# A transformer block on one core: second norm modulated on its turned rows, and the work behind the last block in another order

## The chip, the cores and the metric

The kernel runs on one core of a Trainium2 chip. The metric is device time in microseconds (us) of one execution. Where one execution is profiled, its span (first to last instruction) is a little shorter than its time.

The engines: PE (TensorE, matmuls and turns, that is transposes), DVE (VectorE), ACT (ScalarE), POOL (GpSimd) and SP (SyncE, which here only issues DMAs). Each works through its own instructions in the order of the program; they wait for each other by semaphores. An engine's DMA issues stand in that same order.

## The reference, cut to what matters

2048 tokens of width 512, 32 query heads of 16 that share one key and one value head, and a hidden layer of 1792:

```python
mod = (_silu(c) @ w_mod).reshape(c.shape[0], 6, 1, -1)
sa, ca, ga, sb, cb, gb = (mod[:, 0], mod[:, 1], mod[:, 2], mod[:, 3], mod[:, 4], mod[:, 5])
h = _layernorm(x, axis=-1) * (1 + ca) + sa
x = x + ga * _A_ref(h, A_wq, A_wk, A_wv, A_wo)     # attention, softmax over all keys
h = _layernorm(x, axis=-1) * (1 + cb) + sb
x = x + gb * _B_ref(h, B_w1, B_w2)                 # relu(h @ w1) @ w2
return x
```

The change is about the second norm's `(1 + cb)` and `sb`, one number of each per column of the 512, and about what follows it for the last tokens.

## The kernel before

All arithmetic is float32. Where two operands are multiplied in the faster format (`float32r`), each is split into a high and a low part, and three products are added (`thrice`, line 536: high by high, high by low, low by high). `split` (line 272) makes the parts of a staged value: ACT copies the high part, POOL subtracts it to leave the low one.

**The head** (up to about 130 us) loads x and the weights, makes the six rows of the modulation, the first norm, the keys and values, and the first maxima. `mod_all` (line 218) makes one row of the modulation: PE multiplies silu(c) by a sixth of w_mod into a bank, ACT copies it to `mrow`, PE multiplies by a matrix of constants that adds the parts up and spreads the sum over all partitions, and ACT copies it out (line 225). For sb and cb this gives `sbr` and `cbr`, 128 x 512 each. For the first norm there is another way, `mod_col` (line 228): PE turns `mrow`, and a DVE reduction leaves in `cols` one number per partition and group of 128 columns. `tr1` uses those as scale and shift as turned rows leave their bank.

**The loop** goes over 8 blocks of 256 tokens by 4 groups of 8 heads, so 32 units, each of 16 tiles of keys. For each tile PE makes scores (`scores`, line 773), ACT takes exp, and PE multiplies by the values into the bank `ps_pv`. Maxima of a later unit (`max_of`, line 481) run beside them on PE and DVE. A hand-written row of letters (`PARTS`) says in what order PE gets these pieces; the letters `l` and `u` are portions of other work, which `behind(b)` (line 575) gives out: while block b + 1 is in the loop, the output projection, second norm and hidden layer of block b go in small portions into the bank `ps_fill`. In `behind`, POOL normalises two tiles of 128 tokens and multiplies and adds `cbr` and `sbr` (`normed`, lines 544 to 549); PE turns them; `turned_too` (line 580) copies the turned rows out by ACT and puts off `split` to a later place (`put_off`). Pieces of w1 (`w1s`, 512 KB each with both parts, 14 of them, three buffers) come from DRAM, where the head has left them split.

When a unit's values are done, `normalise` (line 782) makes the quotient: ACT copies the bank to `pvs`; numerators and sums are brought to matching partitions by DMA (`num`, `den`), DVE takes the reciprocal and POOL multiplies into `on` (in the profile under line 1005, where it is called, the last unit's under 1016, DVE's reciprocal too). In the last unit POOL copies both, and SP issues four DMAs for `num` and then four for `den` (lines 793 to 800).

**Behind the loop** first come 24 matmuls that are left of block 6's second layer (first tile of 128 tokens). Then `behind_last(7)` (line 651) does block 7, in the order in which it is written:

- it asks for x and three pieces of w1 (`open_block`, `load_w1`); each further piece is asked for when a chunk of the first layer has been given out (line 704) and waits for one of the three buffers
- it splits the heads' output in two halves of two groups each (`parts`, line 674: ACT high, DVE low), and gives PE 12 matmuls of block 6's second tile (`more(12)`)
- per tile of 128 tokens: 12 matmuls of the projection over the four groups, DVE adds x, takes the statistics (`ln_sums`), makes the reciprocal root in small operations on one column per partition (`ln_stats`, lines 253 to 261), and `normed` follows, the first tile on DVE, the second on POOL
- `more(99)` gives PE the other 30 matmuls of block 6, and DVE closes that tile (`close_block`)
- PE turns the normed rows (8 turns), `parts` splits them into `hh` and `hl`, and the first layer follows: 14 chunks of 12 matmuls (`dense1`), and `parts` with relu
- the second layer takes 84 matmuls, both tiles by turns, and DVE closes both tiles at the end.

Of the kernel before, what the change touches and what calls it, by code (L numbers as in the profile page):

```python
# [13 lines left out]
OP = mybir.AluOpType  # L14
# [29 lines left out]
PARTS = "cbcuaucuautcuau", "tbldldladbllbld"  # L44
SYNC = mybir.DependencyInfo(mybir.DependencyClass.Sync, mybir.DependencyReason.DATA)
# [15 lines left out]
def build(tc, nc, cst, sb, ps, dr, x, wq, wk, wv, wo, w1, w2, c, w_mod, out):  # L61
# [64 lines left out]
    cols = cst.tile([P, 2, DC], F32, name="cols")  # L126
    sbr = cst.tile([P, D], F32, name="sbr")
    cbr = cst.tile([P, D], F32, name="cbr")
# [89 lines left out]
    def mod_all(i, dst):  # L218

        pt = ps_fill()  # L220
        row = mod_row(i, pt)
        yield
        pt = ps_fill()
        nc.tensor.matmul(pt, mean, row, start=True, stop=True)
        nc.scalar.activation(dst, pt, AF.Copy, bias=1.0 if i == 4 else 0.0)
        yield
# [317 lines left out]
    def normed(x1, xn, ts, nm, y, eng):  # L544
        for n, t in enumerate(ts):
            eng.tensor_scalar(xn[:, t], x1[:, t], nm[:, n:n + 1], y[:, n:n + 1],
                              op0=OP.add, op1=OP.mult)
            eng.tensor_tensor(xn[:, t], xn[:, t], cbr, op=OP.mult)
            eng.tensor_tensor(xn[:, t], xn[:, t], sbr, op=OP.add)
# [25 lines left out]
    def behind(b):  # L575
# [74 lines left out]

    def behind_last(b):
# [5 lines left out]
        def second(t):  # L657
            pt = ps_fill()
            for d in dense2(b - 1, t, pt):
                on_all(d)  # L660
                yield
            close_block(b - 1, t, pt)

        before = second(1)
# [20 lines left out]
        for t in range(TT):  # L685
            pt = ps_exp()
            run_all(out_proj(pt, oo, t))
            V.tensor_tensor(x1[:, t], pt, x1[:, t], op=OP.add)
            mv = ln_mv(1)
            ln_sums(mv, 0, x1[:, t])  # L690
            normed(x1, xn, [t], *ln_stats(mv, 1, True), V if t == 0 else nc.gpsimd)
        more(99)
# [15 lines left out]
        pts = [ps_max() for t in range(TT)]  # L708
# [64 lines left out]
    def scores(s, ct):  # L773
        u, kt = divmod(s, KT)
        r = slice((ct % 2) * 64, (ct % 2) * 64 + 50)
        pt = ps_exp()
        nc.tensor.matmul(pt, kp[r, kt * P:(kt + 1) * P], qps[u][ct // 2][r], start=True, stop=True)  # L777
        pe = sb.tile([P, 512], F32, name="pe", tag="pe", bufs=11)
        nc.scalar.activation(pe, pt, AF.Exp)  # L779
        pes[s, ct] = pe  # L780

    def normalise(u, pvt):
# [10 lines left out]
        nc.gpsimd.tensor_copy(num, pvs[:, 0:TB])  # L793
        for c in range(4):
            nc.sync.dma_start(num[c * 32 + DH:(c + 1) * 32], pvs[c * 32:c * 32 + DH, TB:])
        if u == NU - 1:

            nc.gpsimd.tensor_copy(den, pvs[:, TB:])
            for c in range(4):
                nc.sync.dma_start(den[c * 32:c * 32 + DH], pvs[c * 32 + DH:(c + 1) * 32, 0:TB])  # L800
            return [partial(nc.vector.reciprocal, den, den), partial(
                nc.gpsimd.tensor_tensor, on[b][:, g], num, den, op=OP.mult)]

        sums, recs = [dr.tile([8, TB], F32, name=n, tag=n, bufs=2) for n in ("sums", "recs")]
# [86 lines left out]
    def first():  # L891
# [12 lines left out]
        for i, dst in (2, gr[:, 0]), (5, gr[:, 1]), (3, sbr), (4, cbr):  # L904
            yield from mod_all(i, dst)
# [61 lines left out]
    for c in range(NU * KT // 2):  # L967
# [47 lines left out]
    for _, end in ends:  # L1015
        end()
    behind_last(NB - 1)
# [26 lines left out]
```

## Time and profile before

| | |
|---|---|
| median of 3 runs | 1718.91 us (1717.03 to 1719.24) |
| the profiled execution | 1718.99 us, span 1717.2 us |
| PE busy | 1682.0 us, 98% of the span |
| DVE / ACT / POOL busy | 1369.4 / 1227.4 / 347.3 us |
| chain of work that ended last | PE 93%, DVE 3%, DMA 1%, ACT 1% |

In the profile a row of the timeline gives a start and a length in us from the span's start, the engine, the line of the code, the operation, what it writes and reads, and in brackets how long the engine stood idle before it and what ended that. Long runs of equal instructions are one row with a count. The granted clock is the share of full speed that TensorE was given. The line of a matmul behind the loop is that of the helper `on_all` (174 and 177), so the tiles' names tell the work apart: `w2r,r` is the second layer, `woh,oh` the projection, `idn,xn` the turns, `hh,w1s` the first layer.

### The profile page before, as it was taken

How to read it: one execution, taken by the hardware profiler on the slowest of the kernel's cores; microseconds unless marked ns; L12 is line 12 of the kernel's file. 1: busy time of each engine (PE TensorE's matmuls, PEld its weight loads, DVE VectorE, ACT ScalarE, POOL GpSimd, SP SyncE). 2: the span in 40 equal slices, each digit the busy share in tenths (PEclk: the TensorE clock that was granted, in tenths of full speed). 3: DMA queues.
4: the chain of work that ended last, by engine and by line, in shares of the span. 5: the costliest groups of instructions: out<-in, count | busy, mean ns of one | idle time of the engine just before them, and what ended most of it. 6: DMA issues, size and time to landing. Idle time of an engine off the chain costs nothing.

```text
span 1717.2 us, 34193 instructions
## 1 busy us (share of the span) xinstructions
PE 1682.0 (98%) x13196; PEld 936.9 (55%) x13196; DVE 1369.4 (80%) x2327; ACT 1227.4 (71%) x2400; POOL 347.3 (20%) x472
## 2 busy tenths in 40 slices
PE   8899999999999999999999999999999999999988
PEld 5444444445654566445654565446654565556567
DVE  7568888888889888888889888888888888886031
ACT  3227888877877778778877787778877787778810
POOL 3102245431101311121102211131113110131110
PEclk9779999999999999999999999999999999999999
DMA  6113543212301032112301131103201131113123
GB/s 247 60 49 97 177 151 119 84 59 71 102 29 58 21 116 65 35 40 84 102 22 41 47 113 40 59 16 108 78 30 45 59 104 30 56 32 105 45 91 121
DMA packets 86513, 129.12 MB, mean 75 GB/s; under 512 B 24964, under 2 KB 52548, under 8 KB 86352
## 3 DMA queue, kind: packets, MB, share of 16 engines
q1 hardware_dynamic: 84664, 126.85, 23.5%
q8 instruction: 106, 1.74, 0.4%
q14 instruction: 55, 0.45, 0.1%
q10 hardware_dynamic: 1688, 0.08, 0.1%
HBM read 99.94 MB, written 24.76 MB: 73 GB/s over the span
## 4 chain that ended last, share of the span: by engine, by line
PE 93%; DVE 3%; DMA 1%; ACT 1%; issue 1%; POOL 0%; SPq 0%; POOLq 0%; DVEq 0%; ACTq 0%
PE ps_pv L961 30%; PE ps_exp L777 21%; PE ps_fill L194 19%; PE ps_max L490 17%; DVE pm L492 1%; PE ps_max L177 1%; PE ps_exp L177 1%; PE ps_fill L177 1%; DMA w1s<-w1dr 1%; PE ps_exp L353 1%; DVE st L241 1%; PE ps_pv L168 1%; PE ps_exp L190 0%; PE ps_exp L328 0%; PE ps_fill L213 0%
## 5 line engine op out<-in xcount | busy, mean ns | idle before, releaser
L492 DVE TENSOR_REDUCE pm<-ps_max 128x1 f32<-128x512 f32 x2048 | 1293.4, 684 | 204.7 <-PE ps_max L490 166.5
L779 ACT ACTIVATE pe<-ps_exp 128x512 f32<-128x512 f32 x2048 | 1081.6, 606 | 319.8 <-PE ps_fill L194 148.3
L490 PE MATMUL ps_max<-kp,qp 48*128 48x512 f32 x2048 | 808.6, 442 | 9.7 <-DVE pm L492 9.5
L777 PE MATMUL ps_exp<-qp,kp 50*128 50x512 f32 x2048 | 723.9, 413 | 1.7 <-ACT pe L779 1.6
L961 PE MATMUL ps_pv<-pe,vt 128*32 128x512 f32 x4096 | 546.2, 605 | 0.0
L490 PEld LDWEIGHTS ps_max<-kp,qp 48*128 48x128 f32 x2048 | 365.1, 186 | 265.9 <-DVE pm L492 235.3
L777 PEld LDWEIGHTS ps_exp<-qp,kp 50*128 50x128 f32 x2048 | 359.9, 185 | 269.3 <-ACT pe L779 176.6
L194 PE MATMUL ps_fill<-w2r,r 64*128 64x512 f32 x1044 | 302.5, 405 | 0.0
L194 PE MATMUL ps_fill<-hh,w1s 64*128 64x256 f32 x1568 | 243.0, 285 | 0.0
L194 PEld LDWEIGHTS ps_fill<-hh,w1s 64*128 64x128 f32 x1568 | 216.6, 186 | 11.6 <-PEq L187 6.7
L194 PEld LDWEIGHTS ps_fill<-w2r,r 64*128 64x128 f32 x1044 | 181.1, 185 | 12.1 <-PEq L187 2.5
L961 PEld LDWEIGHTS ps_pv<-pe,vt 128*32 128x32 f32 x4096 | 80.6, 108 | 141.2 <-issue 120.2
L194 PE MATMUL ps_fill<-hT,wq 64*128 64x256 f32 x416 | 129.5, 408 | 0.0
L274 POOL TENSOR_TENSOR r<-stg,r 128x512 fp32r<-128x512 f32 x49 | 62.8, 1282 | 318.9 <-ACT r L273 318.9
L194 PE MATMUL ps_fill<-hl,w1s 64*128 64x256 f32 x784 | 126.1, 280 | 0.0
L194 PEld LDWEIGHTS ps_fill<-hl,w1s 64*128 64x128 f32 x784 | 105.6, 186 | 0.0
L194 PEld LDWEIGHTS ps_fill<-hT,wq 64*128 64x128 f32 x416 | 69.2, 187 | 3.2
L1005 POOL TENSOR_TENSOR on<-num,den 128x256 f32<-128x256 f32 x31 | 22.8, 735 | 234.9 <-DMA den<-recs 168.5
L793 POOL COPY num<-pvs 128x256 f32<-128x256 f32 x32 | 12.7, 396 | 179.1 <-ACT pvs L789 179.1
L274 POOL TENSOR_TENSOR hl<-stg,hh 128x512 fp32r<-128x512 f32 x14 | 17.9, 1280 | 129.9 <-ACT hh L273 129.9
L281 ACT ACTIVATE stg<-ps_fill 128x512 f32<-128x512 f32 x62 | 38.3, 618 | 0.0
L294 POOL TENSOR_TENSOR x<-stg,x 128x512 f32<-128x512 f32 x14 | 18.0, 1286 | 99.3 <-ACT stg L293 99.3
(160 smaller groups left out, 946.2 us busy)
## 6 DMA issues: line engine op xcount, KB each, us to landing
w1s<-w1dr SPq DMA_DIRECT2D x112, 512.0 KB
qp<-qdr SPq DMA_DIRECT2D x124, 96.0 KB
qdr<-qq SPq DMA_DIRECT2D x45, 256.0 KB
raw<-in_B_w_dram SPq DMA_DIRECT2D x28, 256.0 KB
w1dr<-w1s SPq DMA_DIRECT2D x14, 512.0 KB
wmod<-in_w_mod_dram SPq DMA_DIRECT2D x6, 1024.0 KB
x<-in_A_x_dram SPq DMA_DIRECT2D x8, 512.0 KB
out_dram<-ot SPq DMA_DIRECT2D x16, 256.0 KB
```

Of the source, the lines that this page charges most:

```text
L168: nc.tensor.matmul(pt[:, 0:P], idn, idn, start=True, stop=True)
L177: nc.tensor.matmul(pt, w, a, start=start, stop=stop)
L194: ins = nc.tensor.matmul(pt, w[r], a[r], start=start and h == 1, stop=stop and h == 0)
L274: (eng or nc.gpsimd).tensor_tensor(lo, src, hi.bitcast(F32), op=OP.subtract)
L281: nc.scalar.activation(stg, pt, func, **kw)
L294: nc.gpsimd.tensor_tensor(dst, stg, other, op=OP.add)
L490: nc.tensor.matmul(pt, qps[u][i][r, j * P:(j + 1) * P], kp[r, kb * 512:(kb + 1) * 512], start=True, stop=True)
L492: nc.vector.tensor_reduce(pms[u][:, (i * 2 + hf) * 4 + j, kb:kb + 1], pt, axis=AX.X, op=OP.max)
L777: nc.tensor.matmul(pt, kp[r, kt * P:(kt + 1) * P], qps[u][ct // 2][r], start=True, stop=True)
L779: nc.scalar.activation(pe, pt, AF.Exp)
L961: nc.tensor.matmul(pvt[i * 32:(i + 1) * 32], vt[:, kt], pes.pop((s, i)), start=(kt == 0), stop=(kt == KT - 1))
L1005: due[1]()
```

## The change

**Modulation.** `sbr` and `cbr` go. `mod_all` makes sb and cb by `mod_col` into `cols` (four turns, a DVE reduction, for cb an addition of one) in place of the matmul and ACT's copy. `normed` only subtracts the mean and multiplies by the reciprocal root. The scale and shift come when the rows are turned: in the loop POOL does it in place on ACT's copy, in two halves (`modulate_two`), ahead of `split`; behind the loop ACT reads the bank once for `hh` and DVE once more for a staged value, from which it subtracts `hh` to leave `hl`, in halves of 256 columns.

POOL's rows for a block's second norm in the loop (`xn` the normed rows, `on` a product of the quotient, `stg` the staged value) were, before:

```order
L546 TENSOR_SCALAR xn<-x_21712,nm,y 128x512
L548 TENSOR_TENSOR xn<-xn,cbr 128x512
L549 TENSOR_TENSOR xn<-xn,sbr 128x512
...
L1005 TENSOR_TENSOR on<-num,den 128x256
L274 TENSOR_TENSOR hl<-stg,hh 128x512
```

In the changed kernel POOL's rows at the same place are:

```order
L548 TENSOR_SCALAR xn<-x_21717,nm,y 128x512 x2
L1048 TENSOR_TENSOR on<-num,den 128x256
L556 TENSOR_SCALAR stg<-stg,cols 128x256 x2
L276 TENSOR_TENSOR hl<-stg,hh 128x512
L276 TENSOR_TENSOR ms<-sq,ms 128x32
```

The four full-width operations on the normed rows are gone, and two half-width ones stand before each `hl`, where ACT's copy to `hh` reads their result.

**The last unit's quotient.** POOL copies only `den`, first; its four DMAs and then the four of `num` are issued by SP and ACT in turn; DVE copies `num` and makes the product.

**Behind the loop.** `behind_last` is now a generator. Its first part is given out ahead of the 24 matmuls that are left: x, pieces 0 to 2 of w1 into their buffers, pieces 3 to 10 as 16 halves into buffers of `pe` (exponentials) and `qp` (queries) that are free by then, the split of the first three groups, and the last unit's reciprocal and product. SP's rows from the last quotient on (`w1dr` the pieces of w1 in DRAM, `w1s` their usual buffers) were, before:

```order
L795 DMA num<-pvs 16x256 x4
L800 DMA den<-pvs 16x256 x4
L597 DMA out_dram<-ot 128x512
L530 DMA x_24341<-in_A_x_dram 128x2x512
L516 DMA w1s<-w1dr_113 128x1024
L516 DMA w1s<-w1dr_114 128x1024
L516 DMA w1s<-w1dr_115 128x1024
L571 DMA out_dram<-ot 128x512
L516 DMA w1s<-w1dr_116 128x1024
```

In the changed kernel SP's rows from there on are (`w1x` the halves in freed buffers):

```order
L835 DMA den<-pvs 16x256 x2
L839 DMA num<-pvs 16x256 x2
L532 DMA x_24315<-in_A_x_dram 128x2x512
L518 DMA w1s<-w1dr_111 128x1024
L518 DMA w1s<-w1dr_112 128x1024
L518 DMA w1s<-w1dr_113 128x1024
L669 DMA w1x<-w1dr_114 128x512 x2
...
L669 DMA w1x<-w1dr_121 128x512 x2
L612 DMA out_dram<-ot 128x512
```

Eight pieces of w1 have moved ahead of the store of block 6's first tile.

After the 24 matmuls come the last group's split, the projection of both tiles over three groups (18 matmuls, into two banks of `ps_max`), the last group (6), and 30 matmuls of block 6's second tile (`more(30)`), where 12 stood before the projection and 30 behind it. The two tiles' statistics are followed by one run of `ln_stats` for both. The other 12 matmuls (`more(99)`) stand behind the turns. PE's rows from behind the 24 matmuls on were, before:

```order
L177 MATMUL ps_exp<-woh,oh 128x512 x4
L177 MATMUL ps_exp<-wol,oh 128x512 x4
L177 MATMUL ps_exp<-woh,ol 128x512 x4
...
L177 MATMUL ps_fill<-w2r,r_22962 128x512
L174 MATMUL ps_exp<-idn,xn 128x128 x8
L177 MATMUL ps_exp<-hh,w1s 128x256 x8
```

In the changed kernel PE's rows from there on are:

```order
L176 MATMUL ps_max<-woh,oh 128x512 x3
L176 MATMUL ps_max<-wol,oh 128x512 x3
L176 MATMUL ps_max<-woh,ol 128x512 x3
...
L176 MATMUL ps_max<-woh,oh 128x512
L176 MATMUL ps_max<-wol,oh 128x512
L176 MATMUL ps_max<-woh,ol 128x512
...
L173 MATMUL ps_exp<-idn,xn 128x128 x8
L176 MATMUL ps_fill<-w2r,r_22966 128x512 x2
L176 MATMUL ps_fill<-w2r,r_22967 128x512
```

The projection stands in runs of three groups with the fourth behind, and matmuls of the second layer stand between the turns and the first layer.

Block 6's second tile is closed after the turned rows have left their banks. Chunks 0 to 2 of the first layer ask for pieces 11 to 13. The second layer does the first tile whole and closes it, and then the second.

The diff, cut to its core:

```diff
@@ mod_all
-        nc.tensor.matmul(pt, mean, row, start=True, stop=True)
-        nc.scalar.activation(dst, pt, AF.Copy, bias=1.0 if i == 4 else 0.0)
+        if dst is None:
+            mod_col(row, i - 1, i == 4, pt)
+        else:
+            nc.tensor.matmul(pt, mean, row, start=True, stop=True)
+            nc.scalar.activation(dst, pt, AF.Copy)
@@ normed
             eng.tensor_scalar(xn[:, t], x1[:, t], nm[:, n:n + 1], y[:, n:n + 1],
                               op0=OP.add, op1=OP.mult)
-            eng.tensor_tensor(xn[:, t], xn[:, t], cbr, op=OP.mult)
-            eng.tensor_tensor(xn[:, t], xn[:, t], sbr, op=OP.add)
+
+    def modulate(dst, src, k, eng):
+        scale, shift = cols[:, 3, k:k + 1], cols[:, 2, k:k + 1]
+        if eng is nc.scalar:
+            eng.activation(dst, src, AF.Identity, bias=shift, scale=scale)
+        else:
+            eng.tensor_scalar(dst, src, scale, shift, op0=OP.mult, op1=OP.add)
+
+    def modulate_two(stg, k2):
+        for k in range(2):
+            v = stg[:, k * TB:(k + 1) * TB]
+            modulate(v, v, k2 * 2 + k, nc.gpsimd)
@@ turned_too, in the loop
-                    put_off.append(split_psum(flat(parts[0], k2), flat(parts[1], k2), pt))
+                    stg = stage()
+                    nc.scalar.activation(stg, pt, AF.Copy)
+                    put_off.append(partial(modulate_two, stg, k2))
+                    put_off.append(partial(split, flat(parts[0], k2), flat(parts[1], k2), stg))
@@ behind_last
+        ahead += [spare_w1(f, "pe", NPE, nc.sync) for f in range(3, 8)]
+        ahead += [spare_w1(f, "qp", 6, nc.sync) for f in range(8, 11)]
...
-        for k2 in range(DC // 2):
-            parts(flat(oo[0], k2), flat(oo[1], k2), flat(on[b], k2))
-        more(12)
+        parts(flat(oo[0], 0), flat(oo[1], 0), flat(on[b], 0))
+        parts(oo[0][:, 2], oo[1][:, 2], on[b][:, 2])
+        for _, end in ends:
+            end()
+        yield
+        parts(oo[0][:, 3], oo[1][:, 3], on[b][:, 3])
+        pts = [ps_max() for _ in range(TT)]
+        for t in range(TT):
+            run_all([d for n, d in enumerate(out_proj(pts[t], oo, t)) if n % DC < 3])
+        for t in range(TT):
+            run_all([d for n, d in enumerate(out_proj(pts[t], oo, t)) if n % DC == 3])
+        more(30)
+        mv = ln_mv(TT)
+        for t in range(TT):
+            V.tensor_tensor(x1[:, t], pts[t], x1[:, t], op=OP.add)
+        for t in range(TT):
+            ln_sums(mv, t, x1[:, t])
...
+        nm, y = ln_stats(mv, TT, True)
+        for t, eng in enumerate((V, nc.gpsimd)):
+            normed(x1, xn, [t], nm[:, t:t + 1], y[:, t:t + 1], eng)
...
-            parts(flat(hp[0], k2), flat(hp[1], k2), pt)
+            stg = stage()
+            for n in range(2):
+                k, c = k2 * 2 + n, slice(n * TB, (n + 1) * TB)
+                modulate(hp[0][:, k], pt[:, c], k, nc.scalar)
+                modulate(stg[:, c], pt[:, c], k, V)
+                V.tensor_tensor(hp[1][:, k], stg[:, c], hp[0][:, k].bitcast(F32), op=OP.subtract)
+        more(99)
+        last[0]()
...
-                if f + 3 < FC:
-                    ahead.append(load_w1(f + 3))
+                if f < 3:
+                    ahead.append(load_w1(f + 11))
...
-        for ds in zip(*[dense2(b, t, pts[t]) for t in range(TT)]):
-            for d in ds:
-                on_all(d)
         for t in range(TT):
-            close_block(b, t, pts[t])
+            pt = ps_max()
+            run_all(dense2(b, t, pt))
+            close_block(b, t, pt)
@@ normalise, the last unit
+            nc.gpsimd.tensor_copy(den, pvs[:, TB:])
+            for c in range(4):
+                (nc.sync, nc.scalar)[c % 2].dma_start(
+                    den[c * 32:c * 32 + DH], pvs[c * 32 + DH:(c + 1) * 32, 0:TB])
+            nc.vector.tensor_copy(num, pvs[:, 0:TB])
+            for c in range(4):
+                (nc.sync, nc.scalar)[c % 2].dma_start(
+                    num[c * 32 + DH:(c + 1) * 32], pvs[c * 32:c * 32 + DH, TB:])
+            return [partial(nc.vector.reciprocal, den, den), partial(
+                nc.vector.tensor_tensor, on[b][:, g], num, den, op=OP.mult)]
@@ behind the loop
+    tail = behind_last(NB - 1)
+    next(tail)
     for part in itertools.chain([portion], others, (p for g in carried for p in g)):
         for d in part:
             on_all(d)
     in_turn(put_off)
-    for _, end in ends:
-        end()
-    behind_last(NB - 1)
+    run(tail)
```

More of the change, by code (lines that the diff above doesn't have):

```diff
@@ L123, in build @@
     make_identity(nc, idn)
-    cols = cst.tile([P, 2, DC], F32, name="cols")
-    sbr = cst.tile([P, D], F32, name="sbr")
-    cbr = cst.tile([P, D], F32, name="cbr")
+    cols = cst.tile([P, 4, DC], F32, name="cols")
     kp = cst.tile([P, S], F32R, name="kp")
@@ L649, in behind, with spare_w1 @@
         carried.append(first_half)
+    def spare_w1(f, tag, bufs, eng):
+        both = [sb.tile([P, DC, P], F32R, name="w1x", tag=tag, bufs=bufs) for _ in range(2)]
+        for n in range(2):
+            eng.dma_start(both[n].bitcast(F32), w1dr[f].bitcast(F32)[:, n])
+        return both
     def behind_last(b):
@@ L777, in scores @@
         nc.tensor.matmul(pt, kp[r, kt * P:(kt + 1) * P], qps[u][ct // 2][r], start=True, stop=True)
-        pe = sb.tile([P, 512], F32, name="pe", tag="pe", bufs=11)
+        pe = sb.tile([P, 512], F32, name="pe", tag="pe", bufs=NPE)
         nc.scalar.activation(pe, pt, AF.Exp)
@@ L795, in normalise @@
             nc.sync.dma_start(num[c * 32 + DH:(c + 1) * 32], pvs[c * 32:c * 32 + DH, TB:])
[L796 to L802, printed above, removed]
         sums, recs = [dr.tile([8, TB], F32, name=n, tag=n, bufs=2) for n in ("sums", "recs")]
@@ L903, in first @@
         yield from qproj_now(0, 0, ps_fill, True, None, TB)
-        for i, dst in (2, gr[:, 0]), (5, gr[:, 1]), (3, sbr), (4, cbr):
+        for i, dst in (2, gr[:, 0]), (5, gr[:, 1]), (3, None), (4, None):
             yield from mod_all(i, dst)
```

15 lines of the change are left out of this document (5 added, 10 removed).

## The prediction, made before the changed kernel was timed

> **What bounds the kernel now.** I read the windows by stage first, then TensorE's timeline in the last 80 us, then the rows that its waits name. In the windows (start:end, length, busy time of PE, PEld, DVE, ACT and POOL, granted clock, DMA share, GB/s) the loop and the stretch behind it differ:
>
> ```profile
> 340.00:700.00 360.00, 358.92 (x3052) 200.49 (x3050) 316.44 (x526) 281.57 (x554) 66.16 (x91) 1.00 0.20 62
> 1636.00:1693.20 57.20, 47.44 (x267) 40.88 (x268) 18.02 (x47) 7.12 (x12) 6.35 (x7) 0.94 0.45 150
> 1660.00:1664.00 4.00, 0.62 (x3) 0.62 (x4) 0.37 (x1) 0.00 (x0) 3.17 (x3) 0.89 0.17 66
> 1664.00:1668.00 4.00, 3.94 (x18) 3.41 (x17) 1.38 (x2) 1.19 (x2) 0.00 (x0) 0.50 0.00 0
> ```
>
> In the loop PE is busy 358.92 of 360 us at full clock: an edit there on another engine is worth nothing while it keeps up. Behind the loop PE loses 9.8 of 57.2 us, and after a hole at 1660 it runs at half clock. PE's timeline there (start, length, last column the wait in front and who ended it):
>
> ```profile
> 1635.93 5.78 PE L177 MATMUL ps_fill<-w2r,r 128*128 128x512 f32 x24
> 1642.46 3.02 PE L177 MATMUL ps_fill<-w2r,r 128*128 128x512 f32 x12 [0.75 <-ACT stg L293]
> 1645.31 0.63 PE L177 MATMUL ps_exp<-woh,oh 128*128 128x512 f32 x2
> 1647.19 0.73 PE L177 MATMUL ps_exp<-woh,oh 128*128 128x512 f32 x2 [1.25 <-ACT oh L675]
> ...
> 1659.20 0.27 PE L174 MATMUL ps_exp<-idn,xn 128*128 128x128 f32 x1
> 1663.38 1.75 PE L174 MATMUL ps_exp<-idn,xn 128*128 128x128 f32 x7 [3.91 <-POOL xn L549]
> ...
> 1671.85 1.21 PE L177 MATMUL ps_exp<-hh,w1s 128*128 128x256 f32 x8
> ...
> 1678.38 1.12 PE L177 MATMUL ps_exp<-hh,w1s 128*128 128x256 f32 x8
> ...
> 1679.83 1.12 PE L177 MATMUL ps_exp<-hh,w1s 128*128 128x256 f32 x8
> ...
> 1693.12 19.76 PE L177 MATMUL ps_max<-w2r,r 128*128 128x512 f32 x84
> ```
>
> Three holes (bank of the second layer, heads of the last group, normed rows), then the first layer: 14 chunks of 12 matmuls, one per piece of w1. The two chunks at 1678.38 and 1679.83 had no wait, so a chunk is 1.45 us; a 512-wide matmul is 19.55/84 = 0.233 us (1693.12 to where DVE's addition behind it starts, 1712.69, next part).
>
> **The change part by part.** Times are start to start, so that the pipeline's refill is in them.
>
> *Bank and heads.* Before, 24 fills from 1635.93 last 24 x 0.233 = 5.6 us, to 1641.5; the next bank opens at 1642.46: 0.9 lost. Two projection matmuls from 1645.31 end at 1645.78, the third starts at 1647.19: 1.4 lost. Now the projection's 18 matmuls of three groups follow the 24 fills, in another bank, and the first gap is gone. Will the operands be there at 1641.5? The rows that time it (DVE and ACT rows, then SP's issues):
>
> ```profile
> 1643.60 1.75 DVE L1016 RECIPROCAL den<-den 128x256 f32<-128x256 f32 x1 [43.55 <-DMA den<-pvs]
> 1645.27 0.63 DVE L679 TENSOR_TENSOR ol<-on,oh 128x512 fp32r<-128x512 f32 x1
> 1645.43 1.04 POOL L1016 TENSOR_TENSOR on<-num,den 128x256 f32<-128x256 f32 x1 [1.67 <-DVE den L1016]
> 1637.27 2.44 SPq L795 DMA_DIRECT2D num<-pvs  x4
> 1639.81 2.42 SPq L800 DMA_DIRECT2D den<-pvs  x4
> ```
>
> Eight issues in a row on SP take 4.9 us, and den, the later, lands at 1643.5. Now den goes first and SP and ACT take two of each four: den is issued by 1638.5 and num by 1639.7; with the same 1.3 us from the end of issue to use, they land near 1639.8 and 1641. The new wait: ACT issues DMAs, so its copy of three groups stands behind them until 1639.7; ACT oh (0.63 for two groups) ends at 1640.3, DVE's ol at about 1641.0, the third group at 1641.4. In time. Then DVE's reciprocal (1.75) to 1643.2 and the product on DVE, some 0.4 instead of POOL's 1.04, then oh and ol of the last group, 0.4 each: 1644.5. PE wants them after 18 x 0.233, at 1645.7. Gain 0.9 + 1.4 = 2.3.
>
> *Normed rows.* Before, the first turn would end at 1659.3 and PE restarts at 1663.38: 4.05 lost, plus the half clock after it: 1663.38 to 1671.85 is 8.47 us for 7 turns and 3 chunks, which at full clock take 7 x 0.125 (half of their 0.25) + 3 x 1.45 = 5.2. Lost: 3.3. Rows of the chain:
>
> ```profile
> 1649.80 0.69 DVE L688 TENSOR_TENSOR x<-ps_exp,x 128x512 f32<-128x512 f32 x1 [1.94 <-PE ps_exp L177]
> 1651.47 0.15 DVE L253 TENSOR_SCALAR ve<-mv 128x1 f32<-128x1 f32 x1
> 1653.85 0.55 DVE L546 TENSOR_SCALAR xn<-x,nm,y 128x512 f32<-128x512 f32 x1
> 1659.88 0.77 POOL L546 TENSOR_SCALAR xn<-x,nm,y 128x512 f32<-128x512 f32 x1 [13.40 <-DVE nm L261]
> 1662.07 1.26 POOL L549 TENSOR_TENSOR xn<-xn,sbr 128x512 f32<-128x512 f32 x1
> ```
>
> Now both tiles share one run of small operations (1651.47 to 1653.85, 2.4 us, once instead of twice), and the multiplication and addition per tile (1.26 each on POOL) go. From the projection's end at 1641.5 + 24 x 0.233 = 1647.1: the second addition ends at 1648.1, two statistics of 0.9 (1650.5 to 1651.4) at 1649.9, small operations at 1652.3, POOL's xn at 1653.2. Cover: 30 fills, 7.0 us, to 1654.1. No hole, 0.9 to spare, and with no hole of this size no half clock. Gain 4.05 + 3.3 = 7.35.
>
> *Modulation on leaving the bank.* New: per half bank ACT writes hh, DVE the staged value and then hl. Nearest rows, 512 wide (ACT, DVE):
>
> ```profile
> L335 ACT ACTIVATE hT<-ps_exp,cols x14: 767/777/780, 14.8 to 68.3; 128x512 f32<-128x512 f32 x14
> L332 DVE TENSOR_SCALAR hT<-ps_exp,cols x1: 811/811/811, 14.8 to 14.8; 128x512 f32<-128x512 f32 x1
> ```
>
> At 256 wide I estimate 0.47 and 0.5, and 0.4 for the subtraction. Cover: the last 12 fills, 2.8 us, between the turns' end (1655.1) and the first chunk (1657.9). ACT and DVE side by side on one bank: the last hh is there at 1657, cost 0. One behind the other: the fourth hh comes some 3.7 us after the bank is full at 1654.9, 1658.6, where PE wants it at 1658.3, and the last hl at about 1659.6 just in time. That costs 0.5 with hand-overs; if hand-overs are twice my 0.06, 1.2. In before DVE reads a bank only behind ACT, because it subtracts ACT's result, so no row shows the first case; I take 0.5, the nearer to what the rows show.
>
> [...]
>
> *Pieces of w1.* From 1671.85 to 1693.12 are 11 chunks: 21.27 against 11 x 1.45 = 15.95: 5.3 lost to fetching. SP's issues, and the rates then, at the kernel's start, and its buffers:
>
> ```profile
> 1668.36 19.43 SPq L516 DMA_DIRECT2D w1s<-w1dr  x11
> 1668.00:1692.00 24.00, 20.19 (x149) 18.91 (x149) 4.15 (x6) 3.58 (x6) 0.00 (x0) 0.96 0.75 241
> 4.00:30.00 26.00, 22.16 (x133) 15.71 (x132) 19.66 (x59) 8.83 (x17) 11.05 (x32) 1.00 1.06 390
> ```
>
> Before, each piece waited for one of three buffers. By the profile's list of issues a piece is 512 KB:
>
> ```profile
> w1s<-w1dr SPq DMA_DIRECT2D x112, 512.0 KB
> ```
>
> Now x, as large, 3 whole pieces and 16 half pieces, 12 x 0.524 = 6.3 MB, are issued in a row from 1639.7, when the last pe and qp readers are through (1636). At 390 GB/s they take 16 us, to 1657; even at 241 GB/s 26 us, to 1667. The eleventh piece is wanted at 1658.4 + 10 x 1.45 = 1672.9. The last three reuse w1s from 1660 on and are wanted from 1674. Behind them on SP stand only stores. Gain 5.3.
>
> *The end.* Two additions of one after the other become one:
>
> ```profile
> 1712.69 1.29 DVE L570 TENSOR_TENSOR ot<-ps_max,x 128x512 f32<-128x512 f32 x2 [18.05 <-PE ps_max L177]
> ```
>
> The first tile is closed under the second's matmuls: gain 0.6.
>
> *The loop.* POOL loses four operations of 1.26 per block and gains four halves of about 0.45. New: ACT's hh waits for POOL's modulation, and the exponentials stand behind it on ACT. In before (ACT, ACT, POOL of one block):
>
> ```profile
> 1155.24 0.60 ACT L281 ACTIVATE stg<-ps_exp 128x512 f32<-128x512 f32 x1 [0.66 <-PE ps_max L490]
> 1159.51 0.63 ACT L273 ACTIVATE hh<-stg 128x512 fp32r<-128x512 f32 x1
> 1160.22 1.28 POOL L274 TENSOR_TENSOR hl<-stg,hh 128x512 fp32r<-128x512 f32 x1 [5.16 <-ACT hh L273]
> ```
>
> 3.67 us lie between the staged value and hh, and POOL idles 5.16 us before hl: 1.0 us of work fits. Cost 0.
>
> *The head.* For two rows of the modulation a 512-wide matmul and ACT's copy become four turns, a DVE reduction and, once, an addition.
>
> ```profile
> 94.81 1.12 PE L224 MATMUL ps_fill<-mrow,mean 128*128 128x512 f32 x2 [0.34 <-ACT mrow L215]
> L232 DVE TENSOR_REDUCE cols<-ps_max x2: 175/176/176, 12.1 to 14.6; 128x4 f32<-128x16 f32 x2
> L236 DVE TENSOR_SCALAR cols<-cols x1: 504/504/504, 12.3 to 12.3; 128x4 f32<-128x4 f32 x1
> ```
>
> PE gains about 0.55 twice; DVE, which PE follows soon after, pays 2 x 0.18 + 0.50 = 0.86. Between +1.1 and -0.3 I take 0.5, since DVE has pauses there.
>
> **Sum:** 2.3 + 7.35 + 5.3 + 0.6 + 0.5 - 0.5 = 15.5 us. The profiled execution took 1718.99 (span 1717.2 and 1.79 around it), 0.08 above the median of 1718.91. 1718.99 - 15.5 = **1703.5**.
>
> **The rivals.**
>
> *Leftover waits.* If issues on SP and ACT don't overlap (8 x 0.6 = 4.8 us), ACT is held to 1642.0 and PE waits 1.2; DVE and POOL at once on xn may hold one another (the product's 1.04 on POOL fell beside DVE's ol), 0.6 more than the cover at most, and hand-overs 0.7. Up to 2.5: 1705.5 to 1707. Chance 0.15.
>
> *The fetch stays late* (buffers not free, or a rate under 190 GB/s): the 5.3 come back, 1708.8. The start's 390 GB/s speaks against it. 0.06.
>
> *A hole of 3 us stays* and with it half clock: 3 + 3.3, 1709.8. 0.04.
>
> *The head's clock.* A long half-clock stretch follows soon after the edit there:
>
> ```profile
> 112.00:116.00 4.00, 4.00 (x15) 2.63 (x13) 2.83 (x6) 0.00 (x0) 0.00 (x0) 0.50 0.83 207
> 124.00:128.00 4.00, 4.00 (x16) 2.57 (x16) 1.31 (x2) 3.25 (x7) 0.00 (x0) 0.50 0.00 0
> ```
>
> PE is full, DVE 2.83 of 4. If the shift kept the clock up, 12 us could shrink by 29% (DVE then leads) and 4 by half: 5.5, 1698.0. 0.08.
>
> [...]
>
> *Slower:* ACT behind POOL in the loop. If the two modulations ended over 4.8 us after the staged value instead of about 1 (POOL's product before them waits for a DMA), each of 14 would hold ACT's exponentials and PE; at 1.4 us each, 19.6 less 15.5: 1723. It decides from 1.1 us each. POOL's 5.16 us of idleness speaks against it. 0.02.
>
> **How the numbers follow.** My case has 0.65; the bounds of its unknown costs (0 to 1.2 at the bank, -0.3 to 1.1 in the head) alone reach from 1702.4 to 1705. With most of the leftover waits and part of the head's clock: 1699.5 to 1707.5 for 8 in 10. Outside 0.2% (3.4 us, about what a measurement can tell) every case but the slower one is faster; 0.02 is kept for several of the bad ones together ending within it: 0.96, 0.02, 0.02.
>
> **What would show it.** Right: after 1636 no PE wait over 0.6; first chunk near 1657.9, the 84 matmuls from about 1679; clock 1.00 there; SP's w1x issues before 1650; ACT hh in the loop still followed by idle-free PE. Wrong: PE waits named after oh, xn, w1x or w1s, a half clock after 1636, or ACT idle on POOL in the loop.

## The result and the profile after

| | before | after |
|---|---|---|
| first pair, medians (4 runs each) | 1717.97 us | 1699.36 us, ratio 0.9899 (95% interval 0.9869 to 0.9929) |
| second pair, later (11 and 6 runs) | 1716.40 us | 1700.98 us, ratio 0.9910 (0.9887 to 0.9933) |
| profiled execution of the first pair, span | 1718.99, 1717.2 us | 1701.09, 1699.3 us |

The forecast was 1703.5. To see where 17.9 us of the profiled pair lie, three marks on TensorE's timeline serve: the loop's first scores, the 24 matmuls that are left, the 84 of the second layer. Of before, two rows that the prediction does not have, the first scores and the 30 matmuls of block 6's second tile:

```profile
123.67 2.76 PE L777 MATMUL ps_exp<-qp,kp 50*128 50x512 f32 x5
...
1652.32 7.05 PE L177 MATMUL ps_fill<-w2r,r 128*128 128x512 f32 x30
```

Of after, TensorE's timeline:

```profile
119.36 2.76 PE L815 MATMUL ps_exp<-qp,kp 50*128 50x512 f32 x5
...
1633.17 5.78 PE L176 MATMUL ps_fill<-w2r,r 128*128 128x512 f32 x24
...
1644.27 7.05 PE L176 MATMUL ps_fill<-w2r,r 128*128 128x512 f32 x30
1651.16 1.03 PE L173 MATMUL ps_exp<-idn,xn 128*128 128x128 f32 x8
...
1654.78 0.52 PE L176 MATMUL ps_exp<-hh,w1s 128*128 128x256 f32 x3
1655.68 0.85 PE L176 MATMUL ps_exp<-hh,w1s 128*128 128x256 f32 x5 [0.39 <-ACT hh L554]
...
1659.82 1.12 PE L176 MATMUL ps_exp<-hh,w1x 128*128 128x256 f32 x8
...
1675.58 19.76 PE L176 MATMUL ps_max<-w2r,r 128*128 128x512 f32 x84
```

| stretch | before | after | gain |
|---|---|---|---|
| start to first scores | 123.67 | 119.36 | 4.31 |
| first scores to the 24 matmuls | 1512.26 | 1513.81 | -1.55 |
| the 24 to the 84 | 57.19 | 42.41 | 14.78 |
| the 84 to the end of the span | 24.08 | 23.72 | 0.36 |

Of the three holes of before none is left; the one wait is 0.39 us for `hh` at the bank. The windows of after (columns as in the prediction) show full clock, and 391 GB/s where the pieces of w1 arrive:

```profile
1640.00:1680.00 40.00, 39.61 (x257) 36.00 (x256) 16.41 (x39) 6.75 (x12) 2.00 (x2) 1.00 0.54 202
1650.00:1652.00 2.00, 2.00 (x15) 1.73 (x13) 0.00 (x0) 0.20 (x1) 0.37 (x1) 1.00 1.05 391
```

SP's issues of the eight pieces of w1 into freed buffers, and the rows of DVE, POOL and ACT around the normed rows and the bank:

```profile
1639.31 12.88 SPq L669 DMA_DIRECT2D w1x<-w1dr  x16
```

```profile
1649.27 0.55 DVE L548 TENSOR_SCALAR xn<-x,nm,y 128x512 f32<-128x512 f32 x1
1649.33 1.04 POOL L548 TENSOR_SCALAR xn<-x,nm,y 128x512 f32<-128x512 f32 x1 [8.38 <-DVE nm L263]
1651.80 0.56 ACT L554 ACTIVATE hh<-ps_exp,cols 128x256 fp32r<-128x256 f32 x1 [10.05 <-PE ps_exp L173]
1652.39 0.54 DVE L556 TENSOR_SCALAR stg<-ps_exp,cols 128x256 f32<-128x256 f32 x1 [2.58 <-ACT hh L554]
1652.97 1.02 ACT L554 ACTIVATE hh<-ps_exp,cols 128x256 fp32r<-128x256 f32 x2 [0.61 <-DVE stg L556]
```

POOL ends the normed rows at 1650.37 and TensorE turns them at 1651.16: 0.8 to spare. The last three rows show ACT and DVE taking turns: each waits for the other's read of the bank.

### The profile page after: what moved, and what is told of

The parts are those of the page before. It is cut to its first block, busy times and chain, and to the rows that moved or that the text cites. A ratio compares the mean times of both kernels' runs of the same rounds, so it can differ in the third digit from the quotient of the medians.

```text
span 1699.3 us, 34192 instructions
## 1 busy us (share of the span) xinstructions
PE 1671.2 (98%) x13200; PEld 934.4 (55%) x13200; DVE 1369.8 (81%) x2324; ACT 1227.4 (72%) x2401; POOL 323.5 (19%) x468
## 4 chain that ended last, share of the span: by engine, by line
PE 94%; DVE 3%; DMA 1%; ACT 1%; issue 0%; POOL 0%; SPq 0%; ACTq 0%; DVEq 0%
PE ps_pv L1004 30%; PE ps_exp L815 21%; PE ps_fill L193 18%; PE ps_max L492 17%; DVE pm L494 2%; PE ps_max L176 1%; PE ps_fill L176 1%; PE ps_exp L176 1%; PE ps_exp L355 1%; PE ps_pv L167 1%; DMA wmod<-in_w_mod_dram 0%; PE ps_exp L189 0%; DVE st L243 0%; DMA recs<-rc 0%; PE ps_exp L330 0%
## 5 line engine op out<-in xcount | busy, mean ns | idle before, releaser
L193 PE MATMUL ps_fill<-wol,oh 64*128 64x512 f32 x112 | 36.8, 408 | 0.0
```

Of the source, the lines that this page charges most:

```text
L193: ins = nc.tensor.matmul(pt, w[r], a[r], start=start and h == 1, stop=stop and h == 0)
```

## The experiments

My theory: behind the loop the gain is made of the three holes, the half clock behind the third, and the fetch, as priced; in the head and in the loop the change does next to nothing, and what differs there is the clock and chance. "24 to 84" is the stretch of the table above in each kernel's profile.

| kernel | median us | before beside it | ratio, 95% interval | 24 to 84 | first scores |
|---|---|---|---|---|---|
| changed, w1 in three buffers | 1706.23 | 1718.31 | 0.9924 to 0.9962 | 50.57 | 117.74 |
| before, early w1 | 1711.78 | 1718.31 | 0.9941 to 0.9978 | 51.20 | 123.69 |
| changed, old modulation | 1702.09 | 1718.31 | 0.9883 to 0.9927 | 45.82 | 118.89 |
| changed, 12 as cover | 1703.86 | 1718.31 | 0.9900 to 0.9947 | 46.28 | 124.44 |
| changed, 22 as cover (one run) | 1702.23 | | | 42.72 | 121.84 |
| changed, quotient on SP | 1698.86 | 1713.03 | 0.9895 to 0.9938 | 42.40 | 118.07 |
| changed, banks apart | 1699.43 | 1713.03 | 0.9899 to 0.9936 | 41.68 | 119.42 |
| changed, one warm | 1695.45 | 1713.03 | 0.9872 to 0.9920 | 42.40 | 112.59 |
| changed, wide warm | 1696.43 | 1713.03 | 0.9865 to 0.9916 | 42.40 | 123.11 |
| changed, unaltered again | 1700.98 | 1716.40 | 0.9887 to 0.9933 | 42.42 | 119.34 |
| banks apart, wide warm, chores | 1694.15 | 1716.40 | 0.9832 to 0.9883 | 41.68 | 119.81 |
| the same, more wide warm | 1689.66 | 1716.40 | 0.9807 to 0.9860 | 41.68 | 108.96 |

**The fetch, undone and alone.** Two kernels, each with one side of this edit:

```diff
 changed, w1 in three buffers
-        ahead += [spare_w1(f, "pe", NPE, nc.sync) for f in range(3, 8)]
-        ahead += [spare_w1(f, "qp", 6, nc.sync) for f in range(8, 11)]
...
-                if f < 3:
-                    ahead.append(load_w1(f + 11))
+                if f + 3 < FC:
+                    ahead.append(load_w1(f + 3))
 before, early w1: the same lines with + and - exchanged
```

> The changed kernel with its pieces of w1 fetched as before (three buffers, each further piece asked for behind a chunk). My theory: the first layer runs at the rate of the fetches again, 21.3 us for 11 chunks instead of 15.95, so the time from the first chunk to the 84 matmuls grows by about 5.3 us and the kernel by as much, to about 1704.7. Rival: the three first pieces, which now have their buffers 20 us earlier, and the 12 matmuls of cover hide part of it, and the fetches took long before only because PE's clock was down: 2 us or less.

> The kernel before with only the early fetch of pieces 3 to 10 of w1 into freed buffers. My theory: the terms add up, so it gains the same 5.3 us, about 1712.7, its 84 matmuls starting 5.3 us earlier behind the turns, with the hole of 3.9 us and the half clock as before. Rival: the eight pieces now move while the heads' quotient and x are fetched and lengthen those waits, or the half clock covers part of the fetch: a gain of 3 us or less.

The changed kernel without the early fetch, on TensorE and SP:

```profile
1651.19 0.52 PE L176 MATMUL ps_exp<-hh,w1s 128*128 128x256 f32 x3
...
1657.71 1.21 PE L176 MATMUL ps_exp<-hh,w1s 128*128 128x256 f32 x8 [1.31 <-DMA w1s<-w1dr]
...
1680.16 19.76 PE L176 MATMUL ps_max<-w2r,r 128*128 128x512 f32 x84
```

```profile
1654.15 20.51 SPq L518 DMA_DIRECT2D w1s<-w1dr  x11
```

Before, with the early fetch:

```profile
1637.09 5.78 PE L177 MATMUL ps_fill<-w2r,r 128*128 128x512 f32 x24
...
1666.22 2.50 PE L177 MATMUL ps_exp<-hh,w1s 128*128 128x256 f32 x8
...
1688.29 19.76 PE L177 MATMUL ps_max<-w2r,r 128*128 128x512 f32 x84
```

Both went my way, by more than I said: 24 to 84 grows by 8.16 us in the changed kernel and shrinks by 5.99 in before, where I expected 5.3 both times. The rest of the change is therefore worth 6.62 without the early fetch (57.19 to 50.57) and 8.79 with it (51.20 to 42.41). The two overlap: with three buffers the first layer is bound by the fetch, 28.97 us from first chunk to the 84 (1651.19 to 1680.16) at full clock, with 6.1 us of waits for `w1s`, and a half clock ahead of it costs nothing that the fetch would not cost. My rivals, that the three early pieces hide part, and that the fetch alone is worth 3 us or less in before, are refuted.

**The normed rows and the half clock.** Three kernels that bring the hole back in different sizes: the old modulation (its diff is the change's part "Modulation" backwards), and

```diff
-        more(30)
+        more(12)        # in the other kernel: more(22)
```

> The changed kernel with the old modulation of the second norm (two rows of 512 columns, multiplied and added on the normed rows; POOL splits in the loop as before), all else as changed. My theory: POOL's normed rows come 2.5 us later, of which 0.8 was spare, so a hole of 1.7 to 2.2 us before the turns, without half clock behind it; the 0.4 at the bank comes back; the head is 1.1 us longer: together about 2.4 to 3 us more, 1702. Rival 1: half clock follows a hole of this size too, 3.3 us more, 1705.5. Rival 2: the 2.07 us that the changed kernel loses in its second unit at the wait for w1's raw rows come from the new modulation; then they come back here, and the time is about 1700.

> The changed kernel with 12 matmuls of block 6 ahead of the turns and 30 behind them (30 and 12 before). My theory: PE has work to 1647.1 only and the normed rows come at 1650.4, a hole of 3.3 us; the wait of 0.85 at the first chunk goes; the clock falls to half only after a hole that is longer than some limit between this and 3.9 us, so 2.9 us more, 1702.3. Rival 1: half clock follows, another 3.3 us, 1705.6. Rival 2: the order of the matmuls is worth nothing, since the chain of the norm also shortens when PE does not disturb it: under 1 us.

> The changed kernel with 22 matmuls ahead of the turns and 20 behind. [...]

Old modulation, TensorE's timeline and windows of 2 us:

```profile
1652.01 0.33 PE L175 MATMUL ps_exp<-idn,xn 128*128 128x128 f32 x1 [1.32 <-DVE xn L550]
1653.13 1.75 PE L175 MATMUL ps_exp<-idn,xn 128*128 128x128 f32 x7 [0.79 <-POOL xn L550]
```

```profile
1652.00:1654.00 2.00, 1.20 (x5) 1.01 (x6) 0.00 (x0) 0.00 (x0) 1.08 (x1) 0.77 0.94 326
1654.00:1656.00 2.00, 2.00 (x9) 1.71 (x8) 1.14 (x2) 1.19 (x2) 0.00 (x0) 0.50 0.85 323
1656.00:1658.00 2.00, 2.00 (x9) 1.64 (x8) 0.24 (x1) 0.00 (x0) 0.00 (x0) 0.87 0.03 10
```

Cover of 12, the same two views:

```profile
1652.18 2.31 PE L173 MATMUL ps_exp<-idn,xn 128*128 128x128 f32 x8 [2.66 <-DVE xn L548]
```

```profile
1650.00:1652.00 2.00, 0.00 (x0) 0.00 (x0) 1.72 (x10) 0.00 (x0) 0.36 (x1) 0.99 1.06 399
1652.00:1654.00 2.00, 1.74 (x7) 1.45 (x8) 0.12 (x1) 0.33 (x1) 0.68 (x1) 0.50 1.03 380
1654.00:1656.00 2.00, 2.00 (x9) 1.67 (x8) 1.51 (x3) 1.25 (x3) 0.00 (x0) 0.66 1.07 394
```

Cover of 22:

```profile
1650.72 0.33 PE L173 MATMUL ps_exp<-idn,xn 128*128 128x128 f32 x1 [0.38 <-DVE xn L548]
1651.27 0.98 PE L173 MATMUL ps_exp<-idn,xn 128*128 128x128 f32 x7 [0.22 <-POOL xn L548]
1652.01 4.83 PE L176 MATMUL ps_fill<-w2r,r 128*128 128x512 f32 x20
1656.67 1.12 PE L176 MATMUL ps_exp<-hh,w1s 128*128 128x256 f32 x8
```

24 to 84 grows by 3.41, 3.87 and 0.31 us. The first two holes came nearly as forecast: 2.11 us with the old modulation (1.7 to 2.2 said) and 2.66 with 12 as cover (3.3 said); with 22 it is 0.60. But half clock follows the first two, so my limit "between 3.3 and 3.9" is refuted; rival 1 stands in both, at half its price. With 22 the matmuls behind the turns run at full clock: 20 of them from 1652.01 to 1656.67, 0.233 us each, and the first chunk runs through. How long half clock lasts is estimated from the clock column: a window at half clock counts 2 us, one at 0.77, if it is at full clock for the rest, counts 2 x 0.23 / 0.5 = 0.92. That gives 0.92 + 2 + 0.52 = 3.4 with the old modulation and 0.04 + 2 + 1.36 = 3.4 with 12 as cover. Of before the first and the last window at half clock, with two at 0.50 between them:

```profile
1662.00:1664.00 2.00, 0.62 (x3) 0.62 (x4) 0.00 (x0) 0.00 (x0) 1.26 (x1) 0.79 0.00 0
...
1668.00:1670.00 2.00, 2.00 (x11) 2.00 (x11) 0.00 (x0) 0.00 (x0) 0.00 (x0) 0.51 0.38 76
```

That is 0.84 + 4 + 1.96 = 6.8, twice as long, behind a hole of 3.91 us. So half clock came behind waits of 2.11 us in two pieces (1.32 and 0.79) and behind single ones of 2.66 and 3.91; 0.60 us in two pieces (0.38 and 0.22) did not bring it. Before with early w1 stays down for 6.8 us too, behind 3.92 us. Why these two stayed down twice as long as the others, the runs do not settle.

Rival 2 for the loop falls too. From first scores to the 24 matmuls the kernels with the old modulation in the loop take 1512.26 (before), 1513.40 and 1513.65 us, those with the new one and the head of the changed kernel as it is 1511.04 to 1513.81. What the profiled run of after lost in its second unit is two waits of ACT for w1's raw rows, behind which its exponentials stand; the longer one:

```profile
197.74 0.63 ACT L275 ACTIVATE w1s<-raw 128x512 fp32r<-128x512 f32 x1 [1.20 <-DMA raw<-in_B_w_dram]
```

In the unaltered kernel's second profile one such wait is left, 0.27 us, and the loop takes 1512.43: these waits differ between runs of one kernel, and so they are not the change's.

**The quotient's queues, and the banks.**

```diff
 quotient on SP (both lines)
-                (nc.sync, nc.scalar)[c % 2].dma_start(
+                nc.sync.dma_start(
 banks apart, when both banks are turned
+        for k2 in range(DC // 2):
+            for eng, j in ((nc.scalar, k2), (V, 1 - k2)):
+                pt, stg = banks[j]
+                for n in range(2):
+                    k, c = j * 2 + n, slice(n * TB, (n + 1) * TB)
+                    modulate(hp[0][:, k] if eng is nc.scalar else stg[:, c], pt[:, c], k, eng)
+        for k in range(DC):
+            V.tensor_tensor(hp[1][:, k], banks[k // 2][1][:, k % 2 * TB:(k % 2 + 1) * TB],
+                            hp[0][:, k].bitcast(F32), op=OP.subtract)
```

> The changed kernel with all eight DMAs of the last unit's quotient issued by SP (den's four first), none by ACT. My theory: den is issued 1.2 us later and num 2.4 us later, num lands near 1640.9 on the changed kernel's scale, when the product begins now, and 0.7 us of slack lies before the last group's matmuls; ACT is free earlier for its copies of the other groups. So 0 to 0.3 us on TensorE's timeline, a median within 2 us of the changed kernel's: the split over two queues is not where the gain comes from. Rival: the later num is waited for, 1.2 us or more between the 18 matmuls and the last group's six.

> The changed kernel with ACT and DVE on different banks as the turned rows leave: ACT makes the first bank's two halves of hh while DVE stages the second bank's, then they change places, and DVE's four subtractions come last. My theory: the wait of 0.85 us (0.39 of it named as a wait for hh, the rest the pipeline's refill) is there because ACT and DVE take turns on one bank; apart, the last hh comes about 1 us earlier and the wait goes, so the first chunk runs through and the kernel gains 0.4 to 0.85 us on TensorE's timeline. Rival: the two engines hold one another up at their reads of the turned rows whatever the bank, and nothing changes, or the later hl are now waited for.

With the quotient on SP alone 24 to 84 is 42.40 instead of 42.41: the split over two queues is worth nothing, as I said. That `den` goes first and the 18 matmuls of three groups stand ahead are left as the reasons; neither was tried alone. At the bank, rows of after's second bank, and then ACT's second pair of halves with the banks apart:

```profile
1654.15 0.42 DVE L735 TENSOR_TENSOR hl<-stg,hh 128x256 fp32r<-128x256 f32 x1
1654.49 0.54 DVE L556 TENSOR_SCALAR stg<-ps_exp,cols 128x256 f32<-128x256 f32 x1
1655.07 0.56 ACT L554 ACTIVATE hh<-ps_exp,cols 128x256 fp32r<-128x256 f32 x1 [1.07 <-DVE stg L556]
```

```profile
1652.35 1.02 ACT L554 ACTIVATE hh<-ps_exp,cols 128x256 fp32r<-128x256 f32 x2 [0.51 <-DVE stg L556]
```

The first chunk (1653.81) runs through without a wait, and 24 to 84 falls by 0.73 (0.4 to 0.85 said); a median cannot show so little among runs that spread by several us. Taking turns at one bank did cost: ACT's last `hh` waits 1.07 us for DVE's read. But that read itself stands behind a subtraction of DVE (the row at 1654.15), and this kernel also puts the subtractions last. So 0.73 is the price of both together; the banks alone were not tried.

**The head.** The head of the changed kernel, as it is, reaches the first scores anywhere from 117.74 to 124.44 us (table). What its clock is worth:

```diff
 one warm
-            warm(2, ps_pv)
+            warm(1, ps_pv)
 wide warm
-            warm(2, ps_pv)
+            warm_r(3)    # three float32r matmuls kp[:, 0:P] x kp[:, 0:512] into ps_pv
 and in the last row of HEAD
-        "kmkmkmkmmwmwmwmwmwmwmwmw")
+        "kmkmkmkmwmwmwmwmwmwmwmwmw")
```

> The changed kernel with one warming matmul in place of two at each of nine places of the head. My theory: the spread of the runs and some 3 us of the 17.9 come from the clock in the head, not from the change. In the last stretch before the first scores the clock is at 0.50 and a round (two maxima, two warming matmuls of 128 x 128) takes 1.87 us of TensorE; DVE's two maxima need 1.29. With one warming matmul a round at half clock takes about 1.3, so 7 rounds gain 4 us: 1695.4. Rival: the warming matmuls do keep the clock up at times, and with fewer of them the clock falls earlier or comes back later in the loop: 0 to 4 us more.

> The changed kernel with three warming matmuls of 512 columns (float32r) in place of two of 128 columns (float32) at each of those places, and one more place where TensorE waits 1.2 us for a maximum. My theory: the clock falls there because TensorE idles before that stretch and streams few columns in it; with 1536 columns a round it stays at 1.00, a round takes DVE's 1.29 us and the loop begins at full clock: 4.5 us and up to 3 more, 1692 to 1695. Rival: the clock falls all the same, and the wider matmuls make a round 2 us at half clock: 1 to 3 us slower than the changed kernel.

One window over that stretch, of after and then of the kernel with wide warming matmuls:

```profile
108.00:124.00 16.00, 16.00 (x53) 10.48 (x54) 9.43 (x16) 3.55 (x7) 0.00 (x0) 0.50 0.38 101
```

```profile
112.00:124.00 12.00, 11.74 (x43) 5.87 (x43) 11.35 (x18) 0.36 (x1) 0.00 (x0) 1.00 0.66 163
```

The warming matmuls of two rounds near the end of the stretch (two maxima stand between them), of after, of one warm and of wide warm:

```profile
116.34 1.22 PE L167 MATMUL ps_pv<-idn 128*128 128x128 f32 x4
...
118.22 1.22 PE L167 MATMUL ps_pv<-idn 128*128 128x128 f32 x4
```

```profile
108.84 0.79 PE L167 MATMUL ps_pv<-idn 128*128 128x128 f32 x2
...
110.29 0.79 PE L167 MATMUL ps_pv<-idn 128*128 128x128 f32 x2
```

```profile
118.29 0.95 PE L175 MATMUL ps_pv<-kp 128*128 128x512 f32 x3
...
119.59 0.96 PE L175 MATMUL ps_pv<-kp 128*128 128x512 f32 x3
```

From one start to the next a round takes 1.88 us, 1.45 (1.57 in others) and 1.30. With one warm the clock still falls (0.50 from 108 to 112 us), and the stretch from the first warming matmul to the first scores is 18.90 us instead of 22.10: 3.2, where 4 was expected; the median is as forecast, with help from the clock earlier on (its profiled run begins the stretch 3.6 us earlier than after's). With wide matmuls the clock holds and the stretch is 18.83, and the loop begins at full clock (1.00 from 124 to 132 us); but the earlier stretches at half clock stay, and its profiled run had more of them than after (mean clock 0.77 from 40 to 100 us, 0.89 in after; first scores at 123.11). So the median, 1696.43, stays above the 1692 to 1695 that I gave.

**A version that beats both.** It has the banks apart, the wide warming matmuls, the chores' loads ahead of the quotient's DMAs (`next(todo, None)` before the loop over `ends`), and wide warming matmuls where TensorE waits 1.26 us in the head:

```diff
+        if b:
+            warm_r(4)            # in kv, ahead of the turns of vT
         pv = ps_exp()
...
+            if b > 1 and k == 0:
+                warm_r(4)        # in tr1_now, ahead of the turns of x
             pt = ps_exp()
```

> The changed kernel with four additions: ACT and DVE on different banks, the three wide warming matmuls in the head, four more of them ahead of the values' turns and of the turned x of the later blocks (TensorE waits 1.26 us there), and the chores' loads issued ahead of the quotient's DMAs in the loop. My theory: 0.7 at the banks, 4 to 5 in the head's last stretch, up to 5 more where the head's earlier half clock goes, up to 2 in the second unit: 1689, with the runs closer together because the clock no longer falls in the head. Rival: the added matmuls delay what they stand before, and the chores' order costs elsewhere: no better than the variant with wide warming matmuls alone, 1696.

> The same without the four additional warming matmuls ahead of the turns: ACT and DVE on different banks, three wide warming matmuls at the ten places, the chores' loads ahead. My theory: 0.7 and up to 2 us better than the variant with wide warming matmuls alone, about 1694, and 3 to 5 worse than with the additional ones. Rival: the additional ones do nothing, the two are equal.

> The changed kernel once more, unaltered, beside the kernel before on one chip. My theory: the stretch from the 24 matmuls that are left to the 84 of the second layer repeats to 0.1 us (42.4), the head and with it the whole time differ by several us with the granted clock, and the median lies 14 to 18 us below that of before. Rival: the 17.9 us of the profiled pair are the change's own, head included, and return in each pair.

The full version takes 1689.66 us (1685.56 to 1690.68) where the changed kernel, beside it on the same chip, takes 1700.98; the one without the additional matmuls 1694.15. These medians are as forecast. The runs are not closer together, as I had said: they spread by 5.1 us, those of the changed kernel by 5.8. Of the full version's profiled run, the fastest of its four, TensorE's row and the span with the mean clock:

```profile
108.96 0.95 PE L830 MATMUL ps_exp<-qp,kp 50*128 50x512 f32 x3
```

```profile
core 0: 1683.8 us, clock 1.000
```

The first scores come 10.4 us earlier than in after. The chores' order shows no effect of its own: first scores to the 24 matmuls takes 1511.34 and 1509.43 us in the two versions with it and 1509.16 with wide warm alone.

## Why the prediction was right, point by point

| term | forecast | measured |
|---|---|---|
| bank and heads | 2.3 | 2.4 (24 to the 30 matmuls, 13.5 without the 12 before, 11.1 after) |
| normed rows and half clock | 7.35 | 7.5 (the 30 matmuls to the fourth chunk: 19.53 before, 12.7 after without the 12 matmuls that have moved there, so 6.8; and the bank's 0.73, which after pays in this stretch) |
| modulation at the bank | -0.5 | -0.73 (banks apart and subtractions last) |
| pieces of w1, 11 chunks | 5.3 | 5.5 (21.27 against 15.76 from 1659.82 to 1675.58) |
| end | 0.6 | 0.36 |
| head | 0.5 | 1.1 |
| loop | 0 | 0 within the profiles' spread |
| sum | 15.5 | 16.2 (14.78 + 0.36 + 1.1) |

*Behind the loop* the mechanisms came as said, most within 0.3 us: clock 1.00, the 84 matmuls 42.41 us after the 24 (1635.93 + 43.1 was said), POOL's normed rows 0.8 us early (0.9 said). One sign that I had named did not come: the issues of `w1x` end at 1652.19 (1654.95 on before's scale, by the start of the 24), not before 1650. It cost nothing, since TensorE never waits for `w1x`: the first piece is used at 1659.82. The prediction's 19.55 us for the 84 matmuls is 19.57 by its own rows, which leaves 0.233 as it is. The row for the last addition but one shows that the first tile's closing is hidden as forecast:

```profile
1685.64 0.69 DVE L582 TENSOR_TENSOR ot<-ps_max,x 128x512 f32<-128x512 f32 x1 [8.53 <-PE ps_max L176]
1695.38 0.69 DVE L582 TENSOR_TENSOR ot<-ps_max,x 128x512 f32<-128x512 f32 x1 [9.05 <-PE ps_max L176]
```

From the last additions' start to the end of the span is 4.51 before and 3.92 after, the forecast 0.6; but from the 84 to that addition is 19.57 before and 19.80 after, which I had not counted.

*In the loop* ACT never waits for POOL's scale and shift (no such wait from 300 to 1630 us), so that the cost of 0 and its reason hold.

*At the bank* I weighed "side by side, cost 0" against "one behind the other, 0.5", and the second is what the rows show; with hand-overs and the subtractions between the reads it is 0.73, inside the range given. ACT's waits for DVE's reads of the bank, 0.61 and 1.07 us, become one of 0.51 when the two work on different banks and the subtractions come last.

*The head* was mis-sized. The edit itself, from the first matmul or turn of sb's row to the warming matmul: before 94.81 to 101.23, after 91.97 to 97.26.

```profile
91.97 0.66 PE L233 MATMUL ps_fill<-idn,mrow 128*128 128x128 f32 x4 [0.34 <-ACT mrow L214]
...
97.26 0.71 PE L167 MATMUL ps_pv<-idn 128*128 128x128 f32 x4
```

```profile
101.23 0.71 PE L168 MATMUL ps_pv<-idn 128*128 128x128 f32 x4
```

6.42 against 5.29, a gain of 1.1, the upper bound: DVE's reductions stood on nobody's path. The other 3.2 us of the head's 4.31 are not the edit's. The kernel with the old modulation has the head of before, with the same 6.42 us, and yet reaches the first scores at 118.89; its mean clock from 40 to 100 us was 0.89, as in after, and 0.77 in before. The head of the changed kernel, as it is, varies by 6.7 us from profile to profile. So the sum that the runs support is 16.2, between the two pairs' differences of medians, 18.6 and 15.4.

The first pair's median fell 0.14 us below the low end of my range. Its four runs lie between 1697.42 and 1705.99, the two fastest with mean clocks of 0.990 and 0.991, the slowest with 0.984. I put what lies beyond 16.2 down to the clock in the head, but only profiled runs show where the clock was down, so this is argued, not shown. My range counted what the change might do to that clock, not what the clock does by itself in either kernel; how near a median of four runs comes to the forecast is luck within several us. The rival in which the shift keeps the clock up did not come: it is at 0.50 from 108 to 124 us in after too.

*What failed* is a price that the sum did not use: the rival of leftover waits counts them at their own length alone. With 2.11 us of them the half clock came for 3.4 us (old modulation): 24 to 84 grew by 3.41, and by 4.1 if the bank's 0.73, which the old modulation does not pay, is left out on both sides; about 1.7 of that is 3.4 us at half speed. As single prices two terms were wrong as well: the fetch and the half clock overlap, so that each alone is worth less than in company.

## What to carry to other kernels

Prices read along one path add up along that path; before an edit is taken or dropped alone, ask what the next bound in its place is: here the early fetch was worth 6 us behind a half clock and 8 us without it. TensorE's waits can have a second price, the clock: here cover that was 0.6 us short, with full clock behind it, cost 1.0 (0.31 and the bank's 0.73, which it hid), and cover that was 2.1 us short, with 3.4 us at half clock behind it, cost 4.1. And where runs of one kernel spread by several us, look for a stretch in the profile in which TensorE is busy and its clock is down: here wide warming matmuls (three of 512 columns in float32r a round, and one place more) took such a stretch from 22.10 us to 18.83.

## What the runs showed of the hardware that was not expected

- A TensorE that the profile calls busy can stay at half clock: 16.00 of 16 us busy and clock 0.50 from 108 to 124 us in after, with maxima of 48 rows and warming matmuls of 128 columns in float32. Three float32r matmuls of 512 columns a round held it at 1.00 in the same place; whether the columns, the format or the one more place did it was not tried apart.
- Run time follows the mean granted clock: 39 runs of the kernel before lie between 1711.0 us (clock 0.991) and 1723.2 us (0.983), with a correlation of -0.96.
- DVE and POOL each took longer when both worked on the two halves of `xn`: POOL's `xn<-x,nm,y` took 0.77 us in the loop, while DVE reduced banks, and 1.04 beside DVE's row of the same kind (after); with the old modulation, both at once, a multiplication took DVE 1.06 and POOL 1.58, where in before, one behind the other, it took 0.69 and 1.26:

```profile
1649.22 1.06 DVE L549 TENSOR_TENSOR xn<-xn,cbr 128x512 f32<-128x512 f32 x1
1649.82 1.58 POOL L549 TENSOR_TENSOR xn<-xn,cbr 128x512 f32<-128x512 f32 x1
```

- Pieces of w1 asked for in a row, as halves of 256 KB, came from DRAM at 391 GB/s (after, 1650 to 1652); the same pieces, asked for whole (512 KB) and one by one as three buffers came free, at 198 to 231 (windows of 10 us of the kernel with three buffers, 1660 to 1680).
